# adaLN block with sliding-window attention: modulation gates, second shift and scale by column-tiled products, GpSimd waits for VectorE's port operations, and a new order

## Chip, cores and metric

The kernel runs on one core of one Trainium2 chip. The metric is the device time of one execution in microseconds (us). TensorE is called PE, VectorE DVE, ScalarE ACT, GpSimd POOL and the queue of SyncE SP, as in the profile; PEld is PE's weight load.

## What is computed

One conditioned transformer block over x of 2048 rows by 640 columns, all tensors bfloat16. Cut to what matters here:

```python
mod = (silu(c) @ w_mod)              # c: 1x640, w_mod: 640 x 3840
sa, ca, ga, sb, cb, gb = six slices of 640 of mod
h = layernorm(x) * (1 + ca) + sa
x = x + ga * A(h)                    # 32 heads of 20, causal window of 256, qkv 640x1920, wo 640x640
h = layernorm(x) * (1 + cb) + sb
x = x + gb * B(h)                    # B(h) = (sigmoid(h @ w_gate) * (h @ w_up)) @ w_down, width 1536
```

Six rows of 640 numbers therefore come from one row vector, silu(c). The shifts (sa, sb) and scales (ca, cb) are applied where the features lie on partitions, so they are needed as columns; the gates (ga, gb) are needed as rows that are alike on all partitions, because the kernel multiplies them into the weights wo and w_down once.

## The kernel before

**Tiling.** The 2048 rows are cut into 8 chunks of 256 (a = 0 to 7), each of two blocks of 128 rows. A chunk goes through: layer norm (`ln1`: statistics and normalization on DVE, a power on POOL), transposition to hT, products with wq, wk and wv (`qkv`), attention, the product with wo (`outproj`), the second layer norm, and the gated MLP (`mlp`). Chunks 0 and 1 are transposed on PE, later ones by transposing transfers; there `modulate` applies scale and shift in place on one of three engines (tags amodu for the first layer norm, bmodu for the second).

**Attention.** A chunk has score sets of four banks of PSUM (tile S, of which there is one). ACT turns each set into exponentials in bfloat16 (tile E, L951), POOL zeroes the masked corners in place (L959, L961), and a burst of column-tiled products with V (tile M, L652) follows for several sets at once, behind the second score set of the next half chunk. DVE transposes the result, divides by the sums (L1005) and transposes back; the output goes to a buffer doc in HBM and comes back as oT.

**Modulation.** silu(c) is copied to 128 equal columns (`silubc`). The first shift and scale come at the start from `modA`, products whose weights are slices of w_mod and whose moving operand is silubc: each has the wanted number in every one of 64 columns. `mod_cols` does the same for the second shift and scale (25 products of 64 columns each). `mod_bc` makes a gate: silubc is the weight operand and w_mod moves, so that all 128 partitions get the same row, in two halves of 320 columns; DVE copies each half to gbc (L699). Ten products and two copies a gate. gbc scales wo (L1174, tag wos) and, for the second gate, wd (L1109, tag wds). The slices of w_mod lie for this time where wu, wd and hh will be: wm1 in wu, wm2 in hh, wm3 in wd.

**Order.** The whole program is a list of operations. A table, PLAN, holds one code for each: five times its number in program order, plus the number of its engine. `schedule` runs through the table and appends each operation to the list of its engine, so the table fixes the order of every engine, the transfer queues of SP and ACT included; `emit` adds semaphore waits for the dependences. While it runs, `schedule` keeps times from given durations. [...]

```python
            if e == "dve" and o.port:
                st = max(st, free["pool"])
            elif e == "pool":
                st = max(st, portend)
```

These times serve the table's making alone: in the program itself no wait stands behind them.

PE's products of full tiles are recorded at L651, tiled ones (scores with row tiles, E,V with column tiles) at L652, all transfers at L549 or, transposing, L764. A PE or SP queue runs in its listed order and stands where an operand is missing.

Of the kernel before, what the change touches and what calls it, by code (L numbers as in the profile page):

```python
# [80 lines left out]
class Prog:  # L81
# [69 lines left out]
    def schedule(self):  # L151
# [7 lines left out]
        pemode = 0  # L159
        portend = 0.0  # L160
# [31 lines left out]
        for code in PLAN:  # L192
# [5 lines left out]
            if e == "dve" and o.port:  # L198
                st = max(st, free["pool"])
            elif e == "pool":  # L200
                st = max(st, portend)
            if o.isdma:
                st = max(st, bw - QMAX)
# [12 lines left out]
            if e == "dve" and o.port:  # L216
                portend = free[e]
# [119 lines left out]
def c_pe(n):  # L337
# [893 lines left out]
```

## Time and profile before

| | |
|---|---|
| time, median of 3 runs | 334.57 us (333.73 to 336.07) |
| time of the profiled execution | 333.99 us |
| its span in the profile | 332.3 us, mean PE clock 1.00 of full |
| busy PE / PEld / DVE / ACT / POOL | 98% / 70% / 65% / 68% / 56% |
| exponentials (L951) | 90, 169.0 us in all |
| masks (L959, L961) | 174, 143.6 us in all |

The profile is one execution. A group line gives line, engine, operation, tiles as output<-inputs, shape and count, then busy time and mean duration in ns of one, then the idle time just before and what ended it. A line of the chain or the timeline begins with start and duration in us. A releaser in brackets names what the engine waited for. Matmuls overlap, so that the durations of several are more than the time they take together, and a PE that counts as busy may still stand for less than the tail of a matmul.

### The profile page before, as it was taken

The numbers are of one execution on the slowest core, as the hardware profiler recorded it, in microseconds if no ns is written. First come the engines' busy times: TensorE is split into PE (matmuls) and PEld (weight loads), VectorE is DVE, ScalarE is ACT, GpSimd is POOL, SyncE is SP. The second block draws the span as 40 slices with busy tenths as digits, with TensorE's granted clock in tenths as the row PEclk, the third lists the DMA queues.
The fourth block names the chain that finished last, engine by engine and source line by source line (L and its number), as shares of the span: only waits on it lengthen the run. The fifth ranks groups of instructions, "written<-read, shape, count | busy, mean of one in ns | idle before, by whom it ended". The sixth has DMA issues, their size and how long they took to land.

```text
span 332.3 us, 10064 instructions
## 1 busy us (share of the span) xinstructions
PE 324.6 (98%) x4142; PEld 232.7 (70%) x4142; DVE 217.1 (65%) x437; ACT 226.3 (68%) x213; POOL 185.8 (56%) x272
## 2 busy tenths in 40 slices
PE   6998999999999999999999999999999999999997
PEld 2766766566677667667677776776776688788885
DVE  5798999986786759574746486637562776374223
ACT  1397999999796978697777878795888683012210
POOL 5048876888867479656573958294829573010000
DMA  7999999789674612836031312540433013203001
GB/s 243 372 351 309 284 273 210 171 132 148 156 146 93 116 46 68 124 73 121 2 99 31 83 24 49 106 112 3 93 41 101 2 41 96 66 20 61 22 0 59
DMA packets 72695, 37.74 MB, mean 114 GB/s; under 512 B 46538, under 2 KB 71370, under 8 KB 72650
## 3 DMA queue, kind: packets, MB, share of 16 engines
q1 hardware_dynamic: 71200, 35.47, 45.2%
q10 hardware_dynamic: 1450, 1.64, 1.6%
q8 instruction: 32, 0.52, 0.7%
q14 instruction: 13, 0.11, 0.1%
HBM read 20.97 MB, written 5.24 MB: 79 GB/s over the span
## 4 chain that ended last, share of the span: by engine, by line
PE 93%; ACT 2%; DMA 2%; DVE 1%; POOL 1%; issue 1%; SPq 0%; POOLq 0%
PE M L651 76%; PE S L652 9%; PE M L652 6%; ACT E L951 2%; DMA hh<-in_w_mod_dram 2%; PE S L632 1%; DVE hT L773 1%; PE S L651 0%; PE S L643 0%; POOL Tn L572 0%; DVE T L998 0%; DVE QT L831 0%; POOL ident L558 0%; POOL stg L569 0%; SPq L549 0%
## 5 line engine op out<-in xcount | busy, mean ns | idle before, releaser
L951 ACT ACTIVATE E<-S 128x2048 bf16<-128x2048 f32 x90 | 169.0, 1878 | 38.0 <-PE S L652 36.0
L961 POOL TENSOR_SCALAR_AFFINE_SELECT E<-E 128x512 bf16<-128x512 bf16 (+1 forms) x84 | 67.7, 813 | 56.6 <-ACT E L951 56.3
L959 POOL TENSOR_SCALAR_AFFINE_SELECT E<-E 128x512 bf16<-128x512 bf16 (+2 forms) x90 | 75.9, 854 | 17.4 <-ACT E L951 17.2
L651 PE MATMUL M<-h2T,wu 128*128 128x256 bf16 x480 | 68.5, 273 | 0.2 <-DVE T L998 0.2
L651 PE MATMUL M<-h2T,wg 128*128 128x256 bf16 x480 | 67.8, 273 | 0.0
L1128 DVE SCALAR_TENSOR_TENSOR hh<-sig,M 128x512 bf16<-128x512 f32 x48 | 32.4, 678 | 43.1 <-ACT sig L1126 20.2
L651 PE MATMUL M<-wd,hh 128*128 128x320 bf16 (+2 forms) x396 | 57.7, 295 | 0.0
L1126 ACT ACTIVATE sig<-M 128x512 f32<-128x512 f32 x48 | 28.1, 595 | 41.3 <-PE M L651 41.3
L651 PEld LDWEIGHTS M<-h2T,wu 128*128 128x128 bf16 x480 | 44.8, 98 | 10.5 <-issue 3.4
L651 PEld LDWEIGHTS M<-h2T,wg 128*128 128x128 bf16 x480 | 45.0, 98 | 9.4 <-issue 2.5
L651 PEld LDWEIGHTS M<-wd,hh 128*128 128x128 bf16 x396 | 37.4, 98 | 14.0 <-issue 1.1
L652 PE MATMUL S<-QT,KT 20*128 20x256 bf16 (+1 forms) x960 | 35.9, 245 | 0.4
L737 DVE BATCH_NORM_STATS2 st<-x 128x6 f32<-128x320 bf16 x64 | 28.9, 478 | 0.7 <-DMA x<-in_A_x_dram 0.3
L998 DVE STREAM_TRANSPOSE T<-M 128x512 f32<-128x512 f32 x32 | 21.0, 691 | 12.4 <-PE S L652 11.2
L652 PEld LDWEIGHTS S<-QT,KT 20*128 20x128 bf16 x960 | 14.1, 92 | 19.7 <-ACT E L951 15.2
L651 PE MATMUL M<-wq,hT 128*128 128x320 bf16 x160 | 27.4, 299 | 0.5 <-DVE hT L773 0.3
L651 PE MATMUL M<-wk,hT 128*128 128x320 bf16 x160 | 27.4, 300 | 0.0
L1147 DVE TENSOR_TENSOR x<-M,x 128x320 bf16<-128x320 f32 (+2 forms) x33 | 15.5, 473 | 16.2 <-PE M L651 15.8
L651 PE MATMUL M<-wv,hT 128*128 128x320 bf16 x160 | 26.0, 300 | 0.0
L831 DVE CAST stg<-M 128x320 bf16<-128x320 f32 x38 | 17.7, 483 | 10.9 <-PE M L651 10.9
L651 PE MATMUL M<-wo,oT 128*128 128x320 bf16 x160 | 24.6, 300 | 0.0
L742 POOL TENSOR_SCALAR st<-st 128x2 f32<-128x2 f32 x16 | 3.7, 234 | 34.9 <-DVE st L739 34.6
(79 smaller groups left out, 335.3 us busy)
## 6 DMA issues: line engine op xcount, KB each, us to landing
x<-in_A_x_dram SPq DMA_DIRECT2D x23, 160.0 KB
doc<-On SPq DMA_DIRECT2D x64, 40.0 KB
wd<-in_w_mod_dram SPq DMA_DIRECT2D x6, 320.0 KB
wd<-in_B_w_down_dram SPq DMA_DIRECT2D x4, 480.0 KB
wu<-in_w_mod_dram SPq DMA_DIRECT2D x5, 320.0 KB
oT<-doc SPq DMA_DIRECT2D x8, 192.0 KB
out_dram<-x SPq DMA_DIRECT2D x8, 160.0 KB
wg<-in_B_w_gate_dram SPq DMA_DIRECT2D x2, 576.0 KB
```

Of the source, the lines that this page charges most:

```text
L651: return e.matmul(o, l, r, start=st, stop=sp, skip_group_check=True)
L652: return e.matmul(o, l, r, start=st, stop=sp, tile_position=tp, skip_group_check=True)
L737: A("dve", lambda e, g, bi=bi, j=j: e.bn_stats(v(bi * 12 + j * 6, 6), src[bi].ap[:, j * 320:(j + 1) * 320]), 0.48, reads=[src[bi].r()], wr ...
L742: A("pool", lambda e, g: e.tensor_scalar(v(28, n), var(), EPS, None, op0=ALU.add), 0.2, reads=[st.r(("m", bi)) for bi in range(n)], writes ...
L831: return e.tensor_copy(dst(), src())
L951: A("act", lambda e, eng: e.activation(E.ap[:], Sp.ap[:], ACT.Exp, scale=SM_SCALE), 1.876, reads=[Sp.r()], writes=[E.r()], prio=3, tag=f"e ...
L959: return e.affine_select(ap, ap, pattern=[[0, ap.shape[1]], [1, 128]], compare_op=ALU.is_ge, fill=0.0, base=0, channel_multiplier=-1)
L961: return e.affine_select(ap, ap, pattern=[[0, ap.shape[1]], [-1, 128]], compare_op=ALU.is_ge, fill=0.0, base=-1, channel_multiplier=1)
L998: A("dve", lambda e, g, h=h: e.transpose(T1.ap[:, 512 * h:512 * h + 512], X[h].ap), 0.694, reads=[X[h].r()], writes=[T1.r(h)], prio=3.5, t ...
L1126: A("act", lambda e, g, pg=pg, sg=sg: e.activation(sg.ap[:], pg.ap[:], ACT.Tanh, scale=0.5), c_act(512), reads=[pg.r()], writes=[sg.r()], ...
L1128: A("dve", lambda e, g, pu=pu, sg=sg, f0=f0: e.scalar_tensor_tensor(out=hh.ap[:, f0:f0 + 2, :], in0=sg.ap[:].rearrange("p (a b) -> p a b", ...
L1147: A("dve", lambda e, g, ps=ps, bi=bi, c0=c0, n=n: e.tensor_tensor(x1[bi].ap[:, c0:c0 + n], ps.ap[:, 0:n], x1[bi].ap[:, c0:c0 + n], op=ALU. ...
```

## The change

Three things are done together.

1. `mod_bc` and `mod_cols` are replaced by `mod_tiles`. silubc is the weight operand with 32 columns, and a row of 640 is cut into four quarters of 160, one for each column tile of PE, so that quarter j stands on partitions 32j to 32j + 31. One group holds a gate and a shift or scale: 5 x 2 x 4 = 40 products, written as one operation. The gate goes on through `mod_gate`: DVE writes one scaled row of 160 (grow), a transfer takes four partitions of it to a buffer in HBM (gout), and another reads it back to all 128 partitions (gin). Shift and scale are laid out so that a DVE transposition of 32x32 blocks (mt) turns them into columns, which ACT copies out (`mod_turn`). silubc is 64 columns wide instead of 128.
2. Chunk 0's transposes are copied out of PSUM without scale and shift, and `modulate` applies these in place.
3. `schedule` adds to each POOL operation a dependence on the last port operation of DVE that stands ahead of it in the table, so that `emit` sets a semaphore wait for it; the time that the table's making counts for it becomes that operation's end with its latency. PLAN is a new table of 2102 codes (2109 before).

```diff
@@ schedule
             elif e == "pool":
                 st = max(st, portend)
+                if port is not None and port not in o.deps:
+                    o.deps.append(port)
...
             if e == "dve" and o.port:
-                portend = free[e]
+                port, portend = o, st + dur + o.lat
...
 PLAN = [
-    3, 57, 81, 114, 78, 91, 62, 89, 222, 99, 68, 104, 8, 13, 263, 109, 28, 195, 225, 202, 206, 212, 230, 217, 119,
...
-    silubc = sb("silubc", [128, NDT, 128])
+    silubc = sb("silubc", [128, NDT, MW])
...
+    grow = sb("grow", [128, 160])
+    mt = sb("mt", [128, 160], F32)
...
-    def mod_cols(i, c0, ps, prio):
...
-    def mod_bc(i, c0, factor, prio):
...
+    def mod_tiles(parts, prio):
+        ps = Tile(p_M, "modt")
+
+        def fn(e, g):
+            ins = None
+            for kt in range(NDT):
+                for n, (i, c0, turned_) in enumerate(parts):
+                    src = wm_ap[i][:, kt, c0:c0 + D]
+                    for j in range(4):
+                        if turned_:
+                            r = src.rearrange("p (t g c) -> p g t c", g=4, c=32)[:, j]
+                            o = ps.ap[32 * j:32 * j + 32, n * 160:n * 160 + 160].rearrange("p (t c) -> p t c", c=32)
+                        else:
+                            r = src[:, j * 160:j * 160 + 160]
+                            o = ps.ap[32 * j:32 * j + 32, n * 160:n * 160 + 160]
+                        ins = mm(e, o, silubc[:, kt, 0:32], r, kt == 0 and n == 0, kt == NDT - 1, tp=(0, 32 * j))
+            return ins
...
+    def mod_gate(ps, n, factor, prio):
+        g = dram(f"gate{prio}", [4, 160])
+        Rd = R("gdram")
+        A("dve", lambda e, _: e.tensor_scalar(grow[:], ps.ap[:, n * 160:n * 160 + 160], factor, None, op0=ALU.mult),
...
+        dma(lambda: g, lambda: grow[0:128:32, :], 0.05, reads=[R_grow], writes=[Rd], prio=1, tag="gout", dur=0.42)
+        dma(lambda: gbc[:], lambda: g.rearrange("(o a) b -> o (a b)", o=1).to_broadcast([128, D]), 0.45, reads=[Rd], writes=[R_gbc],
+            prio=1, tag="gin", dlat=2.6)
+
+    def mod_turn(dst, ps, n, prio, plus, Rdst):
+        A("dve", lambda e, _: e.transpose(mt[:], ps.ap[:, n * 160:n * 160 + 160]), c_dve(160), reads=[ps.r()], writes=[R_mt], prio=8,
...
+        A("act", lambda e, _: e.activation(dst[:], mt[:].rearrange("p (t c) -> p t c", c=32)[:, :, 0], ACT.Identity, bias=plus), 0.25,
...
@@ pe_transposes
+            if a == 0:
+                evac(lambda dt=dt: dst.ap[:, dt, :], lambda ps=ps: ps.ap[:, 0:256], 256, [ps.r()], [dst.r(dt)], 1, f"{ln}hTe{a}")
+                continue
@@ ln1
             turned[a] = pe_transposes(src, t, scA, shA, [R_mA], 1, a)
+            if a == 0:
+                modulate(t, scA, shA, [R_mA], 1, "a", a, src)
@@ build
-    o1 = mod_bc(1, 0, 1.0, 18)
-    psB = Tile(p_M, "modB")
-    cB, o2 = mod_cols(1, 640, psB, 18)
...
+    psB, o1 = mod_tiles([(1, 0, False), (1, D, True)], 18)
+    mod_gate(psB, 0, 1.0, 18)
+    mod_turn(shB, psB, 1, 18, 0.0, R_shB)
...
-    o3 = mod_bc(3, 0, 0.5, 19)
-    psC = Tile(p_M, "modC")
-    cC, o4 = mod_cols(2, 0, psC, 19)
...
+    psC, o3 = mod_tiles([(3, 0, False), (2, 0, True)], 19)
+    mod_gate(psC, 0, 0.5, 19)
+    mod_turn(scB, psC, 1, 19, 1.0, R_scB)
```

More of the change, by code (lines that the diff above doesn't have):

```diff
@@ L159, in schedule @@
         pemode = 0
+        port = None
         portend = 0.0
@@ L622, in build @@
                                                  op1=ALU.mult), 0.2, reads=[R_cth, R_ccol], writes=[R_siluc], prio=0)
-    A("dve", lambda e, g: e.tensor_copy(silubc[:], siluc[:].unsqueeze(2).to_broadcast([128, NDT, 128])), 0.8,
+    A("dve", lambda e, g: e.tensor_copy(silubc[:], siluc[:].unsqueeze(2).to_broadcast([128, NDT, MW])), 0.45,
       reads=[R_siluc], writes=[R_silubc], prio=0)
@@ L676, in pe_chain @@
         return o
-    def mod_cols(i, c0, ps, prio):
-        ops = []
-        for kt in range(NDT):
-            def fn(e, g, kt=kt):
-                ins = None
-                for cg in range(5):
-                    ins = mm(e, ps.ap[:, cg * MW:cg * MW + MW], wm_ap[i][:, kt, c0 + cg * 128:c0 + cg * 128 + 128],
-                             silubc[:, kt, 0:MW], kt == 0 and cg == 0, kt == NDT - 1)
-                return ins
-            ops.append(A("pe", fn, MW / 2400.0 * 5, reads=[Rm[i][kt], R_silubc], writes=[ps.r()], prio=prio, lat=0.2,
-                         tag="modc"))
-        return lambda: ps.ap[:, 0:5 * MW].rearrange("p (a b) -> p a b", b=MW)[:, :, 0], ops
@@ L691, in mod_bc @@
-    def mod_bc(i, c0, factor, prio):
-        ops = []
-        for half in range(2):
-            ps = Tile(p_M, "modb")
-            pairs = [(lambda kt=kt, half=half, ps=ps: (
-                ps.ap[:, 0:320], silubc[:, kt, :], wm_ap[i][:, kt, c0 + half * 320:c0 + half * 320 + 320]))
-                for kt in range(NDT)]
-            ops.append(pe_chain(ps, 320, pairs, [[Rm[i][kt], R_silubc] for kt in range(NDT)], prio, "modb"))
-            A("dve", lambda e, g, ps=ps, half=half: e.tensor_scalar(gbc[:, half * 320:half * 320 + 320],
-                                                                    ps.ap[:, 0:320], factor, None, op0=ALU.mult),
-              c_dve(320), reads=[ps.r()], writes=[R_gbc], prio=8)
-        return ops
+    def mod_tiles(parts, prio):
[14 more added lines that the diff above has]
+            return ins
+        return ps, A("pe", fn, 0.07 * NDT * len(parts) + 0.03, reads=[Rm[i][kt] for i, _, _ in parts for kt in range(NDT)] + [R_silubc],
+                     writes=[ps.r()], prio=prio, lat=0.2, tag="modt", mode=2)
@@ new lines, in mod_gate @@
+    def mod_gate(ps, n, factor, prio):
+        g = dram(f"gate{prio}", [4, 160])
+        Rd = R("gdram")
+        A("dve", lambda e, _: e.tensor_scalar(grow[:], ps.ap[:, n * 160:n * 160 + 160], factor, None, op0=ALU.mult),
+          c_dve(160), reads=[ps.r()], writes=[R_grow], prio=8, tag="grow")
+        dma(lambda: g, lambda: grow[0:128:32, :], 0.05, reads=[R_grow], writes=[Rd], prio=1, tag="gout", dur=0.42)
+        dma(lambda: gbc[:], lambda: g.rearrange("(o a) b -> o (a b)", o=1).to_broadcast([128, D]), 0.45, reads=[Rd], writes=[R_gbc],
+            prio=1, tag="gin", dlat=2.6)
@@ L704, in build @@
+    def mod_turn(dst, ps, n, prio, plus, Rdst):
+        A("dve", lambda e, _: e.transpose(mt[:], ps.ap[:, n * 160:n * 160 + 160]), c_dve(160), reads=[ps.r()], writes=[R_mt], prio=8,
+          tag="mturn")
+        A("act", lambda e, _: e.activation(dst[:], mt[:].rearrange("p (t c) -> p t c", c=32)[:, :, 0], ACT.Identity, bias=plus), 0.25,
+          reads=[R_mt], writes=[Rdst], prio=8, tag="mturn")
     psA = Tile(p_S, "modA")
@@ L773, in mo @@
                 return e.tensor_scalar(ap, ap, sc[:, dt:dt + 1], sh[:, dt:dt + 1], op0=ALU.mult, op1=ALU.add)
-            A(MOE, mo, {"dve": 0.34, "act": 0.59, "pool": 0.55}, port=True, reads=[dst.r(("t", bi)) for bi in range(2)] + Rmod, writes=[dst.r(dt)],prio=prio, tag=f"{ln}modu{a}")
+            A(MOE, mo, {"dve": 0.34, "act": 0.59, "pool": 0.55}, port=True, reads=([dst.r(("t", bi)) for bi in range(2)] if src is None else []) + Rmod, writes=[dst.r(dt)], prio=prio, tag=f"{ln}modu{a}")
     def pe_transposes(src, dst, sc, sh, Rmod, prio, a, ln="a"):
@@ L1163, in build @@
     qkv(1, 21)
-    o1 = mod_bc(1, 0, 1.0, 18)
-    psB = Tile(p_M, "modB")
-    cB, o2 = mod_cols(1, 640, psB, 18)
-    A("dve", lambda e, g: e.tensor_copy(shB[:], cB()), 0.2, reads=[psB.r()], writes=[R_shB],
-      prio=8)
+    psB, o1 = mod_tiles([(1, 0, False), (1, D, True)], 18)
+    mod_gate(psB, 0, 1.0, 18)
+    mod_turn(shB, psB, 1, 18, 0.0, R_shB)
     for h in range(2):
         load_bulk(wu[:, :, h * 768:h * 768 + 768], B_w_up.rearrange("(t p) f -> p t f", p=128)[:, :, h * 768:h * 768 + 768], R_wu[h],
-                  0.59, 0.8 + 0.2 * h, f"wu{h}", extra=o1 + o2, cuts=(3, 5))
+                  0.59, 0.8 + 0.2 * h, f"wu{h}", extra=[o1], cuts=(3, 5))
     for t in range(NDT):
@@ L1175, in build @@
           reads=[R_wo, R_gbc], writes=[R_wo], prio=20, tag="wos")
-    o3 = mod_bc(3, 0, 0.5, 19)
-    psC = Tile(p_M, "modC")
-    cC, o4 = mod_cols(2, 0, psC, 19)
-    p_hh.init[1].extend(o4)
-    A("dve", lambda e, g: e.tensor_scalar(scB[:], cC(), 1.0, None, op0=ALU.add), 0.2,
-      reads=[psC.r()], writes=[R_scB], prio=8)
+    psC, o3 = mod_tiles([(3, 0, False), (2, 0, True)], 19)
+    p_hh.init[1].append(o3)
+    mod_gate(psC, 0, 0.5, 19)
+    mod_turn(scB, psC, 1, 19, 1.0, R_scB)
     nq = 2
```

5 lines of the change are left out of this document (3 added, 2 removed), and 220 rows, old and new, of the table PLAN.

## The prediction

> **What bounds the kernel now.** I read the page first, then the chain of work that ended last in order of time, then the timeline of the stretch in which the modulation products run.
>
> ```profile
> span 332.3 us, 10064 instructions
> ...
> PE 324.6 (98%) x4142; PEld 232.7 (70%) x4142; DVE 217.1 (65%) x437; ACT 226.3 (68%) x213; POOL 185.8 (56%) x272
> ...
> PE 93%; ACT 2%; DMA 2%; DVE 1%; POOL 1%; issue 1%; SPq 0%; POOLq 0%
> ```
>
> The chain lies on PE for 93%, so what leaves PE's queue leaves the span, and what is put into it lengthens it. The other engines matter only where PE waits for them. The chain in order of time shows what paces PE:
>
> ```profile
> 62.89 0.40 PE S L652 x8
> 63.32 1.89 ACT E L951
> 65.25 0.40 PE S L652 x16
> ...
> 218.32 2.07 PE M L651 x18
> 220.39 0.33 PE S L652 x16
> 220.72 2.07 PE M L651 x18
> 222.80 0.33 PE S L652 x8
> ...
> 277.73 52.12 PE M L651 x448
> ```
>
> Two cycles compete from 18 to 277 us. Each of the 90 score sets (S; their number by the code) must wait until the exponential of the set before (E, L951) has read S: start to start 65.25 - 62.89 = 2.36 us is the shortest cycle. Where PE has more than that to do between two sets, PE sets the cycle: 222.80 - 220.39 = 2.41 us with 18 products. After 277.73 only full products are left. So PE work taken out counts in full wherever the stretch between two score sets stays above 2.36 us, and not below it.
>
> **The change, part by part.**
>
> 1. Products removed. The gate rows (L651, `M<-wu,silubc` and `M<-wd,silubc`, 10 each) and the columns of shB and scB (`M<-silubc,wu`, `M<-silubc,hh`, 25 each) go:
>
> ```profile
> 23.64 0.43 SPq L549 DMA_DIRECT2D hh<-in_w_mod_dram  x1
> ...
> 24.01 0.64 PEld L651 LDWEIGHTS M<-wu,silubc 128*128 128x128 bf16 x5
> ...
> 25.92 0.90 PEld L651 LDWEIGHTS M<-silubc,wu 128*128 128x128 bf16 x25
> ...
> 29.28 0.61 PE L651 MATMUL M<-silubc,hh 128*128 128x64 bf16 x15 [0.96 <-DMA hh<-in_w_mod_dram]
> ```
>
> A matmul's own duration contains a pipelined tail, so I take the spacing of the loads, each of which lasts 0.098 us (the row of wo's loads under 6): (0.64 - 0.098)/4 = 0.136 us for 320 columns and (0.90 - 0.098)/24 = 0.033 us for 64. Removed: 20 x 0.136 + 50 x 0.033 = **4.4 us**.
>
> 2. Products added. Two groups of 40, of 128x32 weights by 160 columns. The nearest rows are the column-tiled E,V products of the same 128*32 shape:
>
> ```profile
> L652 PE MATMUL M<-E,V 128*32 128x256 bf16 (+1 forms) x960 | 22.7, 246 | 0.2
> ```
>
> 22.7/960 = 0.0236 us each. By the code a burst of 64 has half its products with 256 columns and half with 128, 192 on average; 160 columns are 0.0236 x 160/192 = 0.0197 us, and 80 of them **1.6 us**. Bounds: 80 x 0.0236 = 1.9 us if columns do not set the rate, and 80 x 0.136/2 = 5.4 us if four quarters run one after another; I take the lower end, as the E,V rows have the same tiles. The strided read of the columns that are to be turned (five runs of 32) has no row; I give it the same price.
>
> 3. Change of tile shape. In the chain's steady stretch a score set follows full products and the loads pause once:
>
> ```profile
> 211.04 1.64 PEld L651 LDWEIGHTS M<-h2T,wu 128*128 128x128 bf16 x16 [0.21 <-issue]
> ```
>
> 0.21 us is 0.1 more than the spacing (1.64 - 0.098)/15 = 0.10 us of that row. Two groups, in and out: 4 x 0.1 = 0.4 us at most; by the table two changes more than before, 0.2. I take **0.3**. [...] If each of the four changes cost the whole tail beyond the spacing, an estimate of 0.15 us (0.61 - 14 x 0.033 in the row at 29.28), term 3 would be 0.6 and the time 0.3 us longer; the pause above bears out the direction, and less of the size.
>
> 4. The wait for hh. PE stood 0.96 us on the transfer of a slice of w_mod, issued at 23.64 and landed at 29.28. In the new table the second group, which reads this slice and the next, stands far later, behind the second burst of chunk 0 and between the third and fourth score set of chunk 1. **-1.0 us.** What is late next could be the second half of the other slice (wm3): it is listed two score sets ahead of the group, 2 x 2.4 = 4.8 us, and behind the first store of chunk 0's output on SP. As slow as 5.6 us, it would give 0.8 us back; I take none of it, and keep it for the range.
>
> 5. The stretches. Read by the codes (five times the operation's number plus the engine), with the prices above, the old table has 11 stretches between score sets with less PE work than the 2.36 us cycle, 1.5 us short in all; the new one has 6, 0.7 us short. **-0.8 us.** 31 pairs of MLP products also leave the end of the list, behind the last score set, for the middle (62 x 0.10 = 6.2 us by the row under 3); on PE alone this costs and gains nothing.
>
> At the start the copy of silu(c) is half as wide, and chunk 0's transposes are evacuated before mA exists and modulated in place on three engines:
>
> ```profile
> 10.80 1.47 DVE L796 TENSOR_SCALAR hT<-M,mA 128x256 bf16<-128x256 f32 x3
> 10.87 1.02 ACT L795 ACTIVATE hT<-M,mA 128x256 bf16<-128x256 f32 x2 [7.22 <-DVE mA L722]
> ```
>
> ```profile
> L772 ACT ACTIVATE hT<-hT,mA 128x256 bf16<-128x256 bf16 x10 | 5.7, 594 | 0.0
> ...
> L773 DVE TENSOR_SCALAR hT<-hT,mA 128x256 bf16<-128x256 bf16 x11 | 5.2, 504 | 0.0
> ```
>
> Now the last of five pieces is ready 1.47 us after mA; then it is two in a row on ACT, 2 x 0.594 = 1.19. That gives **-0.3 us**, between 0, if PE's fillers are what ends last there, and -0.6, if ACT's second piece (0.594) is taken by a faster engine.
>
> 6. Gates, GpSimd's waits, loads of other engines. The gate goes PSUM -> one DVE row -> HBM -> broadcast read, instead of two DVE operations. With transfers as slow as hh's 5.6 us that is 11.2 us; it is hidden as long as wo and wd are needed later:
>
> ```profile
> L651 PEld LDWEIGHTS M<-wo,oT x160: 95/98/100, 55.8 to 293.2; 128*128 128x128 bf16 x160
> ```
>
> ```profile
> L1109 POOL TENSOR_TENSOR wd<-wd,gbc x2: 1393/1400/1407, 86.8 to 88.7; 128x640 bf16<-128x640 bf16 x2
> ```
>
> wo is first used at 55.8, and the first product stands near 24: about 20 us of cover after the transfers (55.8 - 24.0 - 11.2). wd is not complete until 88.7 even now. [...] SP issues four more small transfers, behind which x and transposes queue; eleven more modulations go to ACT (11 x 0.594 = 6.5 us, ACT stands at 68%): nothing, in the range.
>
> Every GpSimd instruction now waits for the last port operation (normalization, division, modulation, scaling) listed ahead of it on DVE; by the table 45 of them are the first behind such an operation, 28 of these masks, 20 of which stand behind a division or a normalization. Behind it stand the masks, for which the E,V burst waits:
>
> ```profile
> PEld M L652 <- POOL E L959: 0.5, 2, 0.3
> ```
>
> ```profile
> 187.60 0.44 DVE L757 TENSOR_SCALAR x<-x,st 128x640 bf16<-128x640 bf16 x1
> ...
> 203.92 0.77 DVE L757 TENSOR_SCALAR x<-x,st 128x640 bf16<-128x640 bf16 x1
> ...
> 209.28 1.33 PEld L652 LDWEIGHTS M<-E,V 128*32 128x32 bf16 x64 [0.21 <-POOL E L959]
> ```
>
> ```profile
> L757 DVE TENSOR_SCALAR x<-x,st 128x640 bf16<-128x640 bf16 x26 | 15.7, 623 | 11.1 <-POOL st L744 10.9
> ...
> L1005 DVE TENSOR_TENSOR Tn<-T,Dr 128x640 bf16<-128x640 f32 x16 | 13.8, 865 | 0.3
> ```
>
> Beside masks DVE's normalization takes 0.77 instead of 0.44 us. Two of the 16 bursts have no slack for their mask. If those two are held for one division, the cost is 2 x 0.865 = 1.7 us; if the new order puts no such operation ahead of them, 0. I take **+0.7**. [...]
>
> Sum: -4.4 + 1.6 + 0.3 - 1.0 - 0.8 - 0.3 + 0.7 = -3.9 us. The profiled execution took 333.99 us (span 332.3 and 1.7 around it), so **330.1 us**; it lies 0.6 under the median 334.57, to which the change is -1.3%. Within 1% is about what a measurement of this kernel can tell from no change.
>
> **Rivals.**
>
> *Masks pace the bursts: slower.* Place: the E,V bursts. If a port operation, late on DVE, stands ahead of the last mask of each burst, all 16 pay a normalization (0.623): 16 x 0.623 = 10.0 us in place of my 0.7, 330.1 + 9.3 = 339.4. For it: the bursts at 209.28 and elsewhere start as soon as the mask is done, and DVE reads PSUM results that PE delivers late. Against it: the table was ordered with the wait counted. It outweighs the gain from 4.6/16 = 0.29 us a burst.
>
> [...]
>
> *The exponentials take the freed time.* Removed products lie between 24 and 42 us, where the cycle is near 2.4 us. Then 4.4 - 1.9 is not gained: 332.6.
>
> *Quarters do not run together*, so the change does not do what it says: 5.4 instead of 1.6 us, 333.9. The E,V rows speak against it.
>
> *The new order packs better than the stretches show*, by another 3 us: 327.1. PE's busy time hides pauses shorter than a product's tail.
>
> **How the numbers follow.** Forecast 0.53, masks 0.15, exponentials 0.14, broadcast 0.10, quarters 0.04, packing 0.04. The forecast's own range is 328.0 to 331.2 (the start from 0 to -0.6, term 6 from 0 to 1.7, terms 2 and 3 by 0.3, term 4's return of 0.8, term 5's stretches by 0.8). With the exponentials, the quarters and the broadcast, and the packing halfway, the range is 326.8 to 336.6; the masks and the far end of packing stay out. Faster by over 1% (below 331.2): 0.53 + 0.04 = 0.57; slower (above 337.9): 0.15; the rest 0.28.
>
> **What would show it.** Right: 80 `silubc` products on the tiled line within some 0.8 us a group, no wait on hh, PE near 320 us busy, the last E,V burst not later than now by more than 2.5 us although more MLP work stands ahead of it, and waits of PE's loads on masks below 2 us. Wrong: GpSimd idle on DVE ahead of masks with PE idle right behind, DVE idle on the gate's read, or a quarter group of 2 us and more.

## Result and the profile after

The changed kernel takes **332.6 us** (median of 10 runs, 331.76 to 333.3) against 334.73 us for the kernel before in the same comparison: ratio **0.9933** (95% interval 0.9917 to 0.995). By the ratio that is 2.2 us less, where 4.5 us (334.57 to 330.1) had been forecast; the sign was right and the size was half. The page of the changed kernel, with the rows that answer to those of before (L656 and L657 are now the lines of full and tiled products, L971 the exponential, L979 and L981 the masks):

```profile
span 330.3 us, 10115 instructions
...
PE 321.0 (97%) x4151; PEld 230.7 (70%) x4152; DVE 209.3 (63%) x431; ACT 231.7 (70%) x225; POOL 177.6 (54%) x271
...
DMA  7989999999770256568303303234031313112101
...
PE 87%; DMA 4%; POOL 3%; DVE 2%; SPq 1%; issue 1%; ACT 1%; POOLq 0%; DVEq 0%
```

PE is busy 3.6 us less, but the span is only 2.0 us shorter, and the chain that sets the end now lies on PE for 87% instead of 93%: the difference went to transfers, GpSimd and DVE. The row of the DMA engines, one digit for each 8.3 us, shows where: they are 70% busy or more in the first twelve slices, but seldom after that. The waits of PE in that stretch are these (the timeline of the changed kernel; in brackets the idle time just before and what ended it):

```profile
23.14 0.70 PEld L657 LDWEIGHTS M<-wu,silubc 128*32 128x32 bf16 x40
...
39.14 0.45 PE L656 MATMUL M<-wk,hT 128*128 128x320 bf16 x2 [0.89 <-DVE hT L787]
...
40.49 0.10 PEld L657 LDWEIGHTS M<-wd,silubc 128*32 128x32 bf16 x4 [0.26 <-DMA wd<-in_w_mod_dram]
...
41.06 0.11 PEld L657 LDWEIGHTS M<-hh,silubc 128*32 128x32 bf16 x4
...
60.32 0.70 PE L656 MATMUL M<-wq,hT 128*128 128x320 bf16 x4 [1.75 <-DMA QT<-stg]
...
66.95 0.49 DVE L1129 TENSOR_TENSOR wd<-wd,gbc 128x640 bf16<-128x640 bf16 x1 [0.30 <-DMA gbc<-gate]
...
73.53 1.50 PE L657 MATMUL M<-E,V 128*32 128x256 bf16 x64
```

The two groups of 40 products last 0.70 and 0.68 us (41.06 + 0.11 - 40.49). The wait on hh is gone. In its place PE stands 0.89 us for a modulated piece of chunk 2, right behind it 0.26 us for the second half of wm3, and 1.75 us for a staging transpose of QT. The last row is the E,V burst of 64 products that I use as a milestone below: in all 17 kernels with the new order, the changed one included, the span ends 256.5 to 257.5 us after its start (here 330.3 - 73.53 = 256.8). So all but 1 us of what tells their profiled executions apart has happened before it.

### The profile page after: what moved, and what is told of

Read it like the earlier page. It is cut to its first block, busy times and chain, and to the rows that moved or that the text cites. A ratio compares the mean times of both kernels' runs of the same rounds, so it can differ in the third digit from the quotient of the medians.

```text
span 330.3 us, 10115 instructions
## 1 busy us (share of the span) xinstructions
PE 321.0 (97%) x4151; PEld 230.7 (70%) x4152; DVE 209.3 (63%) x431; ACT 231.7 (70%) x225; POOL 177.6 (54%) x271
## 4 chain that ended last, share of the span: by engine, by line
PE 87%; DMA 4%; POOL 3%; DVE 2%; SPq 1%; issue 1%; ACT 1%; POOLq 0%; DVEq 0%
PE M L656 72%; PE S L657 8%; PE M L657 6%; DMA wd<-in_w_mod_dram 2%; DMA oT<-doc 1%; DMA hT<-x 1%; SPq L778 1%; POOL E L979 1%; ACT E L971 1%; POOL x L768 1%; PE S L656 0%; POOL E L981 0%; SPq L554 0%; POOL st L758 0%; DVE wo L1192 0%
## 5 line engine op out<-in xcount | busy, mean ns | idle before, releaser
L971 ACT ACTIVATE E<-S 128x2048 bf16<-128x2048 f32 x90 | 168.9, 1876 | 36.8 <-PE S L657 34.9
L979 POOL TENSOR_SCALAR_AFFINE_SELECT E<-E 128x512 bf16<-128x512 bf16 (+2 forms) x90 | 73.3, 827 | 43.1 <-DVE Tn L1025 18.4
L981 POOL TENSOR_SCALAR_AFFINE_SELECT E<-E 128x512 bf16<-128x512 bf16 (+1 forms) x84 | 65.8, 795 | 22.3 <-ACT E L971 11.1
L656 PE MATMUL M<-h2T,wu 128*128 128x256 bf16 x480 | 70.2, 273 | 0.0
L656 PE MATMUL M<-h2T,wg 128*128 128x256 bf16 x480 | 67.7, 273 | 0.0
L656 PE MATMUL M<-wd,hh 128*128 128x320 bf16 (+2 forms) x396 | 58.5, 295 | 0.0
L656 PEld LDWEIGHTS M<-h2T,wu 128*128 128x128 bf16 x480 | 44.5, 98 | 11.3 <-issue 3.8
L656 PEld LDWEIGHTS M<-h2T,wg 128*128 128x128 bf16 x480 | 45.9, 98 | 8.0 <-issue 1.1
L656 PEld LDWEIGHTS M<-wd,hh 128*128 128x128 bf16 x396 | 37.2, 98 | 13.9 <-issue 0.8
L657 PE MATMUL S<-QT,KT 20*128 20x256 bf16 (+1 forms) x960 | 35.9, 245 | 0.2 <-ACT QT L850 0.2
L851 DVE CAST stg<-M 128x320 bf16<-128x320 f32 x44 | 20.9, 483 | 15.0 <-PE M L656 14.8
L656 PE MATMUL M<-wk,hT 128*128 128x320 bf16 x160 | 27.6, 300 | 1.1 <-DVE hT L787 0.9
L656 PE MATMUL M<-wq,hT 128*128 128x320 bf16 x160 | 26.5, 299 | 2.1 <-DMA QT<-stg 1.7
L657 PEld LDWEIGHTS S<-QT,KT 20*128 20x128 bf16 x960 | 14.0, 92 | 19.5 <-ACT E L971 13.3
L656 PE MATMUL M<-wv,hT 128*128 128x320 bf16 x160 | 26.7, 299 | 0.0
L656 PE MATMUL M<-wo,oT 128*128 128x320 bf16 x160 | 25.1, 300 | 0.3 <-DMA oT<-doc 0.3
L657 PEld LDWEIGHTS M<-E,V 128*32 128x32 bf16 x960 | 20.1, 97 | 4.2 <-issue 2.5
```

The source lines that it names most:

```text
L656: return e.matmul(o, l, r, start=st, stop=sp, skip_group_check=True)
L657: return e.matmul(o, l, r, start=st, stop=sp, tile_position=tp, skip_group_check=True)
L851: return e.tensor_copy(dst(), src())
L971: A("act", lambda e, eng: e.activation(E.ap[:], Sp.ap[:], ACT.Exp, scale=SM_SCALE), 1.876, reads=[Sp.r()], writes=[E.r()], prio=3, tag=f"e ...
L979: return e.affine_select(ap, ap, pattern=[[0, ap.shape[1]], [1, 128]], compare_op=ALU.is_ge, fill=0.0, base=0, channel_multiplier=-1)
L981: return e.affine_select(ap, ap, pattern=[[0, ap.shape[1]], [-1, 128]], compare_op=ALU.is_ge, fill=0.0, base=-1, channel_multiplier=1)
```

## Experiments

**1. GpSimd's waits.** First the changed kernel without the waits, everything else as it is (`port` is the code's mark on DVE's normalizations, modulations, divisions and scalings):

```diff
-                if port is not None and port not in o.deps:
-                    o.deps.append(port)
```

> The changed kernel without the semaphore waits of GpSimd on the port operations; order, buffers and everything else as changed. Theory 1 (two new waits of PE in the stretch from 38 to 61 us, 0.9 us on a modulated piece of chunk 2 and 1.75 us on a staging buffer, took back what was gained elsewhere; the waits of GpSimd cost PE nothing): no change against the changed kernel, ratio to before 0.993 within 0.002. Theory 2 (GpSimd's waits, some 40 us of its idle time, hold modulations and normalizations that PE needs): about 2 us faster, ratio 0.987.

Measured: 335.28 us, ratio to the kernel before 1.0014 (0.9997 to 1.0032). Without its waits the new order with its cheaper products gains nothing; the waits, which I had booked as a cost of 0.7 us, **save 2.7 us** (0.0081 of 334.7). The timeline of this kernel (its lines stand two lower) shows how:

```profile
25.74 2.00 POOL L977 TENSOR_SCALAR_AFFINE_SELECT E<-E 128x2048 bf16<-128x2048 bf16 x1
25.81 2.25 DVE L769 TENSOR_SCALAR x<-x,st 128x640 bf16<-128x640 bf16 x1 [0.16 <-POOL st L756]
...
28.58 0.40 PE L654 MATMUL M<-ident,stg 128*128 128x128 bf16 x4 [0.94 <-DVE grow L704]
...
76.25 1.50 PE L655 MATMUL M<-E,V 128*32 128x256 bf16 x64
```

And the same place in the changed kernel:

```profile
25.29 0.45 DVE L771 TENSOR_SCALAR x<-x,st 128x640 bf16<-128x640 bf16 x1 [0.17 <-POOL st L758]
...
25.88 2.00 POOL L979 TENSOR_SCALAR_AFFINE_SELECT E<-E 128x2048 bf16<-128x2048 bf16 x1 [0.62 <-DVE x L771]
```

Here a mask of 2.00 us starts 0.07 us ahead of DVE's normalization, and the normalization takes 2.25 instead of 0.45 us and ends 0.3 us after the mask. How the one holds the other these rows do not show. DVE works in order, so the row of the gate (grow) comes late and PE stands 0.94 us for it. With the wait GpSimd idles 0.62 us instead, and PE does not wait for that mask. This is one place of several: without the waits PE also stands 1.50 us (0.89 with them) for the modulated piece of chunk 2 and 0.63 us (none) for V, which were not followed back to a mask, and the milestone comes 2.7 us later (76.25 against 73.53). The prediction gave no price to this case, in which the mask starts first, DVE is the engine that takes longer and the wait saves.

Two more kernels ask whether this belongs to the new order, and which operations carry it. The kernel before, with its own table and the waits alone:

```diff
             elif e == "pool":
                 st = max(st, portend)
+                if port is not None and port not in o.deps:
+                    o.deps.append(port)
...
-                portend = free[e]
+                port, portend = o, free[e]
```

> The kernel before with nothing of the change but the waits: each POOL operation depends on the last port operation of DVE ahead of it in the table; the times that the table's making counts stay as they were, and so does the table. Theory 1 (the waits gain by keeping GpSimd's masks off DVE's short normalizations, as 335.3 without them against 332.6 showed in the new order): faster than before by 1 to 3 us, 332 to 333.7, DVE's normalization near 0.45 us each instead of 0.62 on average. Rival (the waits help only where the table was made for them): in the old table 69 GpSimd operations start before the port operation ahead of them has ended, held masks delay bursts: 335.5 to 337.

Measured: 334.16 us, 0.9986 (0.9972 to 1.0), so about 0.5 us saved, and between nothing and 0.9. Its normalizations do shrink as expected, from a mean of 623 ns before to this (group line of that kernel):

```profile
L760 DVE TENSOR_SCALAR x<-x,st 128x640 bf16<-128x640 bf16 x26 | 11.3, 456 | 12.2 <-POOL st L747 12.1
```

Theory 1 had the sign and not the size: 4.4 us of DVE time saved are worth half a us in a kernel whose PE, in the trace from 8 us on, stands for DVE 0.30 us at most. And the waits on normalizations alone, in the changed kernel:

```diff
-                port, portend = o, st + dur + o.lat
+                portend = st + dur + o.lat
+                if o.tag[1:3] == "xh":
+                    port = o
```

> The changed kernel with GpSimd's waits set on DVE's normalizations alone (26 operations), not on divisions, modulations and scalings. Theory 1 (the 2.7 us of the waits come from normalizations, which take 0.45 us alone and up to 2.25 us beside a mask, with PE's operands behind them): 332.3 to 333.2, the normalization near 0.47 us on average, the division near 0.92. Rival (divisions and the first modulations carry it): 334.3 or more. A third way (holding masks for divisions costs something that the normalizations pay back): 331.5.

Measured: 333.25 us, 0.9957 (0.9935 to 0.998): about 1.9 of the 2.7 us (1.0014 - 0.9957). Group lines of this kernel:

```profile
L1027 DVE TENSOR_TENSOR Tn<-T,Dr 128x640 bf16<-128x640 f32 x16 | 14.6, 913 | 0.3
...
L773 DVE TENSOR_SCALAR x<-x,st 128x640 bf16<-128x640 bf16 x26 | 11.6, 468 | 8.0 <-POOL st L760 7.9
```

The normalizations are as short as with all waits, the divisions as long as without any. Normalizations carry most of it; whether divisions carry the rest, 0.8 us, lies within the intervals.

**2. The products.** The changed kernel with `mod_bc` and `mod_cols` back in place of `mod_tiles`, in the new order otherwise; the second gate's products stand behind the last scaling of wo:

```diff
-    psB, o1 = mod_tiles([(1, 0, False), (1, D, True)], 18)
-    mod_gate(psB, 0, 1.0, 18)
-    mod_turn(shB, psB, 1, 18, 0.0, R_shB)
+    o1 = mod_bc(1, 0, 1.0, 18, gbc, R_gbc)
+    cB, o2 = mod_cols(1, 640, psB, 18)
...
```

> The changed kernel with the old untiled products: ten broadcast products and two copies for a gate, 25 products for a shift or scale, no way through HBM; the new order otherwise, with the second gate's products moved behind the last scaling of wo and the first load of w_down behind them. Theory 1 with the forecast's price of the products: 2.5 us slower than the changed kernel, 335.1 us, ratio 1.001. Rival: the products' gain is hidden behind other waits in that stretch and is worth 1 us or less: 333.6 us, ratio 0.996 or lower.

Measured: 338.44 us, 1.0112 (1.0079 to 1.0145), but this number is not that of the products: a w_down load of 480 KB stood ahead of the loads of oT on SP's queue, and the timeline shows PE standing for them:

```profile
59.81 3.87 PE L654 MATMUL M<-wo,oT 128*128 128x320 bf16 x15 [4.07 <-DMA oT<-doc]
```

So once more, with that load behind the last staging transpose of chunk 2 (SP's queue, in order):

```diff
-    qkt2, wd, oT_0, oT_0, wg0, x11, qkt2, qkt2, qkt2, atr4
+    qkt2, oT_0, oT_0, wg0, x11, qkt2, qkt2, qkt2, wd, atr4
```

> The first kernel with the old products, with one more move: the w_down load that then stood ahead of the two loads of oT goes behind the last staging transpose of chunk 2 on SP's queue, so that the old products are all that is left of the difference. Theory 1 (terms 1 to 3 of the prediction hold, 4.4 - 1.6 - 0.3 = 2.5 us for the products): 332.6 + 2.5 = 335.1, between 334.3 and 336, the wait of 4 us on oT<-doc gone. Rival (the products lie beside waits in the changed kernel, so that taking them out gains little): 333.2 or less.

Measured: **333.41 us**, 0.9949 (0.9932 to 0.9965), 0.5 us (by the ratios) above the changed kernel with overlapping intervals: much nearer the rival (333.2 or less) than theory 1 (334.3 to 336). The loads of its products, in the timeline:

```profile
23.55 1.22 PEld L654 LDWEIGHTS M<-wu,silubc 128*128 128x128 bf16 x10
24.80 0.90 PEld L654 LDWEIGHTS M<-silubc,wu 128*128 128x128 bf16 x25
...
40.85 0.44 PE L654 MATMUL M<-wk,hT 128*128 128x320 bf16 x2 [0.90 <-DVE hT L776]
...
42.13 0.80 PEld L654 LDWEIGHTS M<-silubc,hh 128*128 128x128 bf16 x25 [0.19 <-issue]
52.47 1.32 PEld L654 LDWEIGHTS M<-wd,silubc 128*128 128x128 bf16 x10
...
65.58 1.09 ACT L775 ACTIVATE hT<-hT,mA 128x256 bf16<-128x256 bf16 x2 [0.34 <-DMA hT<-x]
...
68.55 0.40 PE L655 MATMUL S<-QT,KT 20*128 20x256 bf16 x8
...
74.47 1.50 PE L655 MATMUL M<-E,V 128*32 128x256 bf16 x64 [0.27 <-ACT stg L839]
```

The old products take 1.22 + 0.90 + 0.80 + 1.32 = 4.2 us, the new ones 1.4: PE does have 2.9 us less to do, as forecast. But with the old products PE doesn't wait for QT<-stg, and the milestone comes only 0.9 us later (74.47 against 73.53).

**3. The late operands, one by one.** All of the following are the changed kernel with a few codes of PLAN moved; the edits are shown as the order that results on an engine or queue, by tags. On SP's queue x6 to x11 are loads of blocks of x, atr the transposing transfers of a chunk, qkt the staging transposes of its QT and KT, n_ow the stores to doc and oT the loads back, wm2 and wm3 second halves of those slices of w_mod, gout the gate's row on its way to HBM, and wo, wg, wu and wd loads of weights. Two single moves: DVE's normalization of chunk 3 behind the modulation of chunk 2; and on SP's queue the second gate's row (gout) and a w_gate load behind the staging transposes.

```diff
-    DVE: ..., axh3, ..., amodu2, ...
+    DVE: ..., amodu2, axh3, ...
```

> One entry of the table moved: DVE's normalization of a block of chunk 3 comes behind its two modulations of chunk 2 instead of ahead of them. Theory 1: the wait of PE for the modulated piece near 38 to 39 us goes, 0.9 us, ratio 0.9905. Theory 2: no change, 0.993.

```diff
-    SP: oT_0, oT_0, gout, wg0, x11, qkt2, qkt2, qkt2, atr4
+    SP: oT_0, oT_0, x11, qkt2, qkt2, qkt2, gout, wg0, atr4
```

> Two entries of SP's list moved: the second gate's store and a load of w_gate (576 KB) come behind the four staged transposes of chunk 2 instead of ahead of three of them. Theory 1: those transposes are late because loads stand ahead of them, the wait of PE of 1.75 us near 58 to 60 us goes or shrinks, ratio 0.988 to 0.990. Rival: the transposes wait for what they transpose, nothing changes, ratio 0.993, and the wait stands where it was.

Measured: 332.9 us (0.9937, 0.9912 to 0.9962) and 333.01 us (0.9942, 0.9918 to 0.9967). Neither gains. In the first the wait on hT is gone, and this stands in its place, right behind:

```profile
35.32 0.38 SPq L554 DMA_DIRECT2D wd<-in_w_mod_dram  x1
...
41.32 0.25 PE L657 MATMUL M<-wd,silubc 128*32 128x160 bf16 x4 [0.91 <-DMA wd<-in_w_mod_dram]
```

In the second the wait on QT<-stg is gone, as its theory 1 said, but its profiled execution loses more before anything that was moved is issued:

```profile
34.98 0.38 SPq L554 DMA_DIRECT2D wd<-in_w_mod_dram  x1
...
43.05 0.33 PE L657 MATMUL M<-wd,silubc 128*32 128x160 bf16 x4 [1.90 <-DMA wd<-in_w_mod_dram]
```

PE stands for the same transfer, wm3's second half, in both. From its issue to PE's products it takes 6.0 us in the first, 6.1 in the changed kernel (34.39 to 40.49), and 8.1 in the second, although SP's queue has the same order up to there in all three. So a landing can differ by 2 us between executions, and no order of the queue explains that.

Then wm3's second half, the late operand that the prediction had named, issued right behind wm2's; alone, with the DVE move, and with all three moves:

```diff
-    SP: wg0, wm2, atr2, wu0, x6, wg1, gout, atr2, wo, wg1, n_ow_0, wm3, x8
+    SP: wg0, wm2, wm3, atr2, wu0, x6, wg1, gout, atr2, wo, wg1, n_ow_0, x8
```

> The changed kernel with one code of PLAN moved: the issue of the second half of wm3 (the slice of w_mod in wd) goes from behind the first store of chunk 0's output on SP's queue to right behind the second half of wm2, so it is issued some 8 us earlier. Theory 1 (what ate the gain are two late operands that stand one behind the other, the modulated piece of chunk 2 and this half): this half's wait near 40.5 us goes, but the 0.89 us on hT stays, because it ends first; 332.4, within 0.4 us of the changed kernel's 332.6. Theory 2 (the half alone is the bound there): 1 us less, 331.6. Theory 3 (transfers only change places, the earlier half delays chunk 2's transposes and stores): 333.5 or more, with PE waiting longer on hT.

> Both the earlier second half of wm3 and the DVE operation swap (the normalization axh3 behind the modulation amodu2). Theory 1: with both operands early PE stands for neither near 39 to 42 us, and 0.9 to 1.1 us leave the time: 331.6 against 332.6 for the changed kernel. Rival (a third operand, or the next set's exponential, takes the place of the wait): within 0.4 us of the changed kernel. The single moves alone: 332.9 measured for the swap.

> The two moves of the previous kernel and, besides, the row of the second gate (gout) and wg0's transfer behind the last staging transpose of chunk 2 (qkt2) on SP's queue. Theory 1 (late transfers between 37 and 62 us are worth 1.1 + 1.9 us in the changed kernel): 332.6 - 3.0 = 329.6, half a us below the prediction's 330.1. Rival (a wait removed only uncovers the next late transfer): 331.6 or more.

Measured: 333.38 us (0.9966, 0.9944 to 0.9989), 333.08 us (0.9953, 0.9937 to 0.9969) and 332.81 us (0.9945, 0.9921 to 0.997). Alone the early half of wm3 makes chunk 2's piece later, as theory 3 said: chunk 2's transposed block lands 2.45 us later than in the changed kernel (at 35.54 there, at 37.99 here), GpSimd's statistics wait behind it, DVE's axh3 for these, and the piece behind axh3. Timeline of the changed kernel, then of this one:

```profile
35.54 1.09 POOL L787 TENSOR_SCALAR hT<-hT,mA 128x256 bf16<-128x256 bf16 x2 [1.07 <-DMA hT<-x]
```

```profile
37.99 1.09 POOL L787 TENSOR_SCALAR hT<-hT,mA 128x256 bf16<-128x256 bf16 x2 [3.29 <-DMA hT<-x]
...
41.58 0.71 PE L656 MATMUL M<-wk,hT 128*128 128x320 bf16 x2 [3.10 <-DVE hT L787]
```

In the timeline of the second kernel both waits near 40 us are gone, and later operands take their place:

```profile
54.88 2.20 PE L656 MATMUL M<-wo,oT 128*128 128x320 bf16 x15 [2.26 <-DMA oT<-doc]
...
61.51 0.70 PE L656 MATMUL M<-wq,hT 128*128 128x320 bf16 x4 [1.25 <-DMA QT<-stg]
```

With the third move the second of these goes as well, and this is the longest that is left (timeline of the third kernel):

```profile
54.24 2.20 PE L656 MATMUL M<-wo,oT 128*128 128x320 bf16 x15 [1.62 <-DMA oT<-doc]
```

The next kernel takes that away too, and another is the same without the waits of GpSimd:

```diff
-    SP: x9, atr3, wd, atr3, n_ow_0 (4), x10, qkt2, oT_0, oT_0, x11, qkt2, qkt2, qkt2, gout, wg0
+    SP: x9, n_ow_0 (4), atr3, atr3, oT_0, oT_0, qkt2, x10, x11, qkt2, qkt2, qkt2, gout, wg0, wd
```

> The kernel with three moves, and on SP's queue also chunk 3's transposes behind the stores of chunk 0's second half, then the two loads of oT, and behind these the load of x10, KT's staging transpose and the last w_down load for the gap (wd). The three moves left one wait of 1.62 us on oT<-doc at 54.24 us and no other near it. Theory 1 (all that kept the changed kernel from the forecast is operands that come late from transfers in the first 65 us): this wait goes too, and the time is 332.8 - 1.6 = 331.2 or less, within 1.2 us of the forecast 330.1; runs in which the granted clock falls get rare. Rival (each transfer moved ahead only makes another late): within 0.5 us of 332.8, with a wait of 1 us or more on another tile.

> The same order without GpSimd's waits on DVE's port operations. Theory 1 (the waits save by keeping masks off DVE's normalizations and divisions, whatever the transfers do): 2 to 3 us longer than the kernel with all moves, 333.5 or more, and DVE busy longer by 5 us or more. Rival (in the changed kernel the waits gained because they happened to put transfers in a better order): within 0.7 us of the kernel with all moves.

Measured: **335.5 us** (1.0003, 0.9978 to 1.0028) and 337.58 us (1.0088, 1.0057 to 1.0119). The waits of GpSimd are worth 2.8 us here too, so in the new table their gain is the same in two orders of the transfers. The move itself lost. PE stands 1.31 us for QT<-stg again (at 59.48), and 2.19 us ahead of a score set, for the exponential before it, and ACT, in order, stands in front of that exponential for chunk 4's transposed block:

```profile
66.32 1.09 ACT L786 ACTIVATE hT<-hT,mA 128x256 bf16<-128x256 bf16 x2 [2.66 <-DMA hT<-x]
...
69.23 0.40 PE L657 MATMUL S<-QT,KT 20*128 20x256 bf16 x8 [2.19 <-ACT E L971]
```

**4. A block that lands at the same time until its own transposes are moved.** The w_down load moved alone, so that the only difference from the kernel with the old products is the products and the gates' way; then also gout and wg0; then, besides these, the DVE move and wm3's second half right behind chunk 2's transposes, so that all waits of the changed kernel up to 62 us are addressed:

```diff
-    SP: x9, atr3, wd, atr3, ..., qkt2, qkt2, qkt2, atr4
+    SP: x9, atr3, atr3, ..., qkt2, qkt2, qkt2, wd, atr4
```

> The changed kernel with one transfer moved: the 480 KB load of w_down (wd) goes behind the last staging transpose of chunk 2 on SP's queue, where the second kernel with the old products has it. The two then differ in the products and the gates' way alone. Theory 1 (that load makes QT<-stg late): the wait of 1.75 us near 60.3 goes and the time is 331 to 331.8, 1.6 us or more below the old products in the same place (333.4). Theory 2 (PE simply arrives earlier at operands whose transfers set the pace): 332.2 to 333, a wait of 1.2 us or more on QT<-stg stays.

```diff
-    SP: x9, atr3, wd, atr3, ..., gout, wg0, x11, qkt2, qkt2, qkt2, atr4
+    SP: x9, atr3, atr3, ..., x11, qkt2, qkt2, qkt2, gout, wg0, wd, atr4
```

> The same, and the row of the second gate and w_gate's load behind that transpose too. Theory 1 (what stands ahead of the transposes on SP's queue makes them late): no wait on QT<-stg, 330.8 to 331.6. Theory 2: a wait of 1 us or more takes its place on another tile, 332.2 or more.

```diff
     (the last, and)
-    DVE: ..., axh3, ..., amodu2, ...
-    SP: atr2, wo, wg1, n_ow_0, wm3, x8
+    DVE: ..., amodu2, axh3, ...
+    SP: atr2, wm3, wo, wg1, n_ow_0, x8
```

> The same as the last, and near 40 us the normalization axh3 behind the modulation amodu2 on DVE and the second half of wm3 right behind chunk 2's last transpose, ahead of the loads of wo and w_gate. Theory 1 (all waits of the changed kernel between 38 and 62 us go, 3.0 us by the trace): 329.6 to 330.5. Theory 2 (each leaves a late operand behind it): 332 or more.

Measured: 333.21 us (0.9954, 0.9931 to 0.9978), 334.75 us (0.9985, 0.9958 to 1.0012) and 334.22 us (0.9976, 0.9956 to 0.9996). The first reads as the old products do in the same order (0.9954 against 0.9949; in the executions with a mean clock of 0.998 or more, 333.0 against 333.4 us): **of the products' 2.9 us nothing is left that these runs could tell from zero**. Its timeline shows where they went:

```profile
65.42 1.09 ACT L786 ACTIVATE hT<-hT,mA 128x256 bf16<-128x256 bf16 x2 [2.56 <-DMA hT<-x]
...
68.33 0.40 PE L657 MATMUL S<-QT,KT 20*128 20x256 bf16 x8 [2.09 <-ACT E L971]
```

With the old products chunk 4's block starts at 65.58 us, after a wait of 0.34 us; with the new ones at 65.42, after 2.56 us; and the score set behind it starts at 68.55 and 68.33, so that 0.2 of the 2.9 us is left there. In the last kernel no wait over 0.5 us is left before 62 us, and it reads 65.71 and 3.05. ACT, and PE behind it, reach the block 2 to 3 us earlier and find it not landed. The last two kernels therefore move what stands on SP's queue between and ahead of the block's two transposes, with the earlier waits mended and without:

```diff
-    SP: gout, wg0, ..., qkt2, qkt2, qkt2, atr4, wd, atr4, qkt3
+    SP: ..., qkt2, qkt2, qkt2, atr4, atr4, gout, wg0, wd, wd, qkt3
```

> The last kernel (all waits before 62 us mended), with the row of the second gate, w_gate's load and the two w_down loads (480 KB each) behind both transposes of chunk 4 on SP's queue. Theory 1 (chunk 4's block is the gate through which all earlier gains are lost): it lands 1.5 to 2.5 us earlier, near 63.5, ACT waits at most 1.5 us for it, the clock stays at 1.00 more often, and the time is 330 to 331.5, below the changed kernel and near the forecast 330.1. Theory 2 (the transposes are paced by the normalization on GpSimd at 57.3 to 58.2 us and by their own time, whatever stands between them): it lands at 65 or later and the time stays at 333 or more.

> The changed kernel with these four transfers moved and nothing else. Theory 1: QT<-stg is no longer late (1.75 us in the changed kernel), chunk 4's block lands near 63.5 and the time is 331 to 331.8, the waits near 40 us being left. Theory 2: the wait of 1.75 us goes and ACT's wait on hT<-x grows by as much, 332.4 or more.

Measured: 334.28 us (0.9975, 0.9955 to 0.9996) and 334.32 us (0.9983, 0.9961 to 1.0005). The block comes 3 to 4 us earlier (at 61.83 and 62.16), further than theory 1 said, and the time doesn't follow. Timeline of the kernel with the earlier waits mended:

```profile
61.83 1.08 ACT L786 ACTIVATE hT<-hT,mA 128x256 bf16<-128x256 bf16 x2
...
67.81 0.43 PE L656 MATMUL M<-wk,hT 128*128 128x320 bf16 x2 [2.17 <-DMA QT<-stg]
69.51 0.72 PE L656 MATMUL M<-wk,hT 128*128 128x320 bf16 x2 [1.27 <-POOL hT L787]
...
76.94 1.50 PE L657 MATMUL M<-E,V 128*32 128x256 bf16 x64
```

Now QT's staging transpose, behind the two w_down loads, is the late one. So my theory of a single gate fell as well: it is no one transfer, but the row of them. What is shown is that between 38 and 76 us PE runs up to transfers in every order I tried, and that time taken from PE there comes back as a wait. What is open is whether an order exists that avoids it: eleven orders gave 332.8 to 335.5 us, none below the changed kernel. Much of the spread among them is the granted clock, told at the end: in their executions with a mean clock of 0.998 or more their medians lie between 332.1 and 333.6 us (two of them rest on a single execution). I also can't say which part of this is the queue's order and which the load on the DMA engines, which were not told apart; the two landings of wm3's half in one order show that the order is not all.

## Why the prediction was wrong

- **Terms 1 and 2 (products): right on PE, wrong in the sum.** Removed 4.2 us (forecast 4.4), added 1.4 (forecast 1.6). The quarters do run together. Term 3, the change of tile shape, was measured by no run alone.
- **Term 4, and the rule ahead of the terms that "what leaves PE's queue leaves the span", are the step that failed.** The wait for hh went, as said. Then the text asked what is late next, named wm3's second half with a price of 0.8 us, and took none of it. PE stands 0.89 + 0.26 us at that place and 1.75 at 60 us; mend them and it stands elsewhere. Of the products' 2.9 us 0.2 is left at the score set behind chunk 4's block, and without GpSimd's waits the change gives nothing (335.28 us) where the sum without term 6 has 4.6. The sum took time off PE's queue in a stretch where that queue had nearly caught up with the transfers. In the rivals this was seen for the exponentials only. The 332.6 of that rival equals the measured time, but not by its cause, as the next point shows.
- **Term 6 has the wrong sign.** Booked: +0.7, from masks that come late. Measured: -2.7 us. GpSimd's idle time did grow, and the group of waits of the changed kernel shows it on divisions (us in all, times, longest):

```profile
POOL E L979 <- DVE Tn L1025: 18.4, 5, 6.0
```

  but PE's loads waited for masks 1.3 us in all. The row of 0.77 against 0.44 us stood in the prediction; I priced the engine that waits and not the one that is freed.
- The two errors offset each other: without term 6 the forecast sum was -4.6 and the measured one +0.5 us (335.28); with it -3.9 and -2.2. That half of the forecast gain came, and not none of it, is owed to that: it is luck. The range of 326.8 to 336.6 was wide enough for 335.28 as well.
- **The range.** The lower end of the forecast's own range adds up from its terms (328.0). The upper does not: the terms named (0.3 for the start, 1.0 for term 6, 0.3 for terms 2 and 3, 0.8 and 0.8) add 3.2 to 330.1, which is 333.3 and not 331.2, the bound of a 1% gain. The measured 332.6 lies below 333.3 and above 331.2. Packing halfway is 328.6, so that 326.8 doesn't follow from it.
- **Term 5.** The first score set starts at 17.72 instead of 17.84 us, a gain of 0.1, not 0.3. The stretches could not be seen apart from the waits.
- **The tests named.** No wait on hh, 0.7 us a group, PE at 321 us, little wait on masks: all came. The last E,V burst was to come at most 2.5 us later and comes 4.9 later (281.15 against 276.22): 2.4 us too late, the size of the miss.
- **Rivals.** Masks pace the bursts: refuted, as above. The gate's broadcast (chance 0.10): DVE stood 0.30 us for gbc at 66.95 and nothing for the first gate, so no. No run shows the lateness of it that the range up to 336.6 counts, nor how soon such a transfer would land with no other beside it; the nearest row is c_row at the start of the kernel before, 1.2 KB, issued at 0.79 and loaded by PE at 3.02 us. Quarters: no. A better packing: no.

## What to carry to other kernels

Before you book PE work as saved, look at the DMA row of the stretch where it is taken out: here, where transfers were 70% busy or more and operands were used as soon as they landed, 0.2 of 2.9 us was left at chunk 4's block, and mending a wait showed the next one. A wait that keeps an operation of one engine from overlapping one of another is priced on both sides: what the waiting engine loses (GpSimd 0.62 us at the first mask), and what the other, in order, no longer stands for (DVE 1.80 us at one normalization, PE 0.94 us behind it). Take a change of several parts to pieces in both orders (here the waits alone gave 0.5 us in the old table and 2.7 in the new), since a right total can be made of two wrong terms.

## Hardware behaviour that was not expected

While PE stood for a missing operand, or shortly after, the granted clock sometimes fell to half, for 3.4 or 6.8 us. Windows of the kernel in which the w_down load alone was moved; its columns are the window, its length, busy time and count of PE, PEld, DVE, ACT and POOL, the granted clock, DMA share and GB/s (the DMA share of such short windows can read above 1, and nothing is built on it):

```profile
66.50:67.00 0.50, 0.00 (x0) 0.00 (x0) 0.00 (x0) 0.50 (x2) 0.00 (x0) 1.00 1.27 268
...
69.50:70.00 0.50, 0.50 (x4) 0.34 (x3) 0.00 (x0) 0.50 (x3) 0.50 (x2) 0.74 0.74 148
70.00:71.00 1.00, 1.00 (x6) 0.54 (x4) 0.91 (x2) 1.00 (x1) 1.00 (x2) 0.50 0.63 125
...
72.00:73.00 1.00, 1.00 (x5) 0.59 (x4) 0.00 (x0) 0.39 (x1) 1.00 (x3) 0.50 0.50 134
73.00:74.00 1.00, 1.00 (x8) 0.72 (x7) 0.49 (x1) 0.00 (x0) 0.59 (x2) 0.92 0.22 40
```

PE stood 2.09 us up to 68.33, and 1.4 us later its clock is halved: by the clock of the first and the last of these windows, 0.74 and 0.92, from 69.74 to 73.16, which is 3.42 us. In the kernel with gout and the w_gate load moved (experiment 3) it fell inside the stand of 1.90 us that ended at 43.05, after 1.3 us of it:

```profile
42.25:42.50 0.25, 0.00 (x0) 0.00 (x0) 0.00 (x0) 0.00 (x0) 0.25 (x1) 0.89 1.32 380
42.50:42.75 0.25, 0.00 (x0) 0.00 (x0) 0.00 (x0) 0.00 (x0) 0.25 (x1) 0.50 0.89 247
```

Worked out in the same way, the half clock lasts 3.41 to 3.42 us in six of the 19 profiled executions and 6.82 to 6.83 us in three, so here it lasted one or two times 3.4 us. All nine have a stand of PE of 1.9 us or more, which still lasts when the clock falls or ended at most 2.4 us before; of the other ten, two have such a stand (2.26 us in the kernel with two moves, 2.19 in that with four) and no drop, and the 1.75 us of the changed kernel had none either. The same kernel shows it in some executions only: the changed kernel had a mean clock below 0.998 in 1 of 10 runs, the one with four moves in 10 of 12 (median 335.6 us in those, 333.0 in the other two), and the second kernel with the old products, whose longest stand is 0.90 us, in 0 of 9. That the stand is the cause is read from this; no run was made for it alone. A PE that is busy all through loses half of each 3.4 us, 1.7 us, as an estimate from the clock of 0.50. By that estimate the wait of 2.09 us above cost up to 3.8 us (2.09 + 1.7), and the 2.6 us between the two medians of the kernel with four moves go with the lower clock.
